# Value windows of a dilated local attention: 64 scratch planes read by 16 large loads instead of 128 small ones, reciprocals spread by ScalarE, and a new order of all steps

## The chip, the cores and the metric

The kernel runs on one core of one Trainium2 chip. A core has five engines that each work through their own instruction queue in order: TensorE (PE, matrix products; its weight loads are shown as PEld), VectorE (DVE), ScalarE (ACT), GpSimd (POOL), and SyncE (SP), which here only issues DMAs. DMAs move data between the chip's DRAM and the on-chip memory SBUF; matrix products land in PSUM, a small accumulator memory. The metric is the device time of one execution in microseconds.

## The reference

There are 2048 tokens of 512 features, all in bfloat16. After a first layernorm (xn) two branches are computed and joined:

```python
def _A_ref(x, wqkv, wo):                      # H = 32 heads of Dh = 16
    W, dil = 8, 2
    qkv = (x @ wqkv) ...                      # q, k, v per head
    idx = pos[:, None] - off[None, :]         # each token sees itself and 2, 4, ... 14 tokens back
    logits = einsum("bhsd,bhswd->bhsw", q, kg) * scale   # 8 logits per token and head
    logits = where(idx >= 0, logits, -1e9)
    attn = softmax(logits)
    o = einsum("bhsw,bhswd->bhsd", attn, vg)  # weighted sum of 8 shifted values
    return o @ wo

def _B_ref(x, w1, w2, w3, w4):
    h = gelu(layernorm(x) @ w1)
    hs = concat(four quarters of h shifted by 1, -1, 2, -2 tokens) @ w2
    x1 = x + hs
    return x1 + gelu(layernorm(x1) @ w3) @ w4    # F = 1376

xn = layernorm(x);  s = _A_ref(xn, ...);  g = silu(_B_ref(xn, ...));  return x + s * g
```

## The kernel before, in words

Tokens are cut into 16 tiles of 128, four tiles to a chunk, four chunks. Small Python functions, called steps, each issue one piece of work for one tile, chunk or column block. A string ORDER (line 16 and following) lists the names of all steps; at the end of the program the steps are called in that order. Every engine therefore gets its own instructions in the sequence of ORDER, and an instruction that waits holds up everything behind it on the same engine. Nothing reorders it later.

The steps, by name (c is a chunk, i a tile):

- x and w steps (SP): loads of inputs and weights; `xc2`, `xc3` are the 512 KB loads of the x rows of chunks 2 and 3.
- `st`, `rsa`, `rsb`, `rsc`, `xn` (lines 261 to 308): first layernorm. Statistics on DVE, the power of -1/2 on POOL (`rsb`), `-mean*rstd` on DVE (`rsc`), and the normalised rows on ACT (`xn`, line 308; for chunk 0 on DVE). `r2a`, `r2b`: the second layernorm's scale, DVE and POOL.
- `tr`, `xe` (PE transposes, then copies) or `tx` (line 339, a DMA transpose issued by SP): xn turned for the products. Chunks 0 and 1 use PE, chunks 2 and 3 the DMA.
- `qk c.n` (line 393), `qe` (line 399): eight products per chunk for q and k, and their evictions on ACT.
- `v i`, `ve i`, `vst i` (lines 405, 411, 416): values of one tile; ACT evicts them with the features of a head interleaved; POOL issues the store to the DRAM scratch `v_dram`, 2062 rows of 1 KB, the first 14 zero.
- `h i`, `he i`, `hst i` (lines 405, 420, 426): first MLP product, gelu on ACT, DMA transpose issued by SP into `hT`. `pl`, `pr_`: two columns on each side copied by POOL. `mix i` (line 553): the product of the shifted quarters with w2. `xo`, `s3` (DVE), `ra3`, `rb3`, `rc3`, `xm` (ACT), `x1T` (DMA transpose, SP): x1, its layernorm and its turned form.
- `pw c.u` (DVE, line 448), `lg c.u` (PE, line 457): q times k shifted by 2u, and the sum over the 16 features of a head by a product with a 0/1 matrix, for the eight shifts u. PSUM tile `lg` holds 8 x 128 logits for (tile of the chunk, head) on the partitions.
- `mask`, `mx`, `ls`, `ex`, `to`, `sh`, `et`, `ae` (lines 462 to 514): softmax over the eight shifts, then eight PE transposes (`et`) and a copy (`ae`) that bring the weights to partitions (shift within a half, token within 32). In `sh` DVE takes the reciprocals, casts them and multiplies.
- `lv i.half` (line 655): loads of the shifted values of one tile, four DMAs of 128 KB for each half of the shifts, issued by SP, each to 32 partitions. `pr i` (DVE, line 661): values times weights, 4096 elements per partition. `ws i` (PE, line 670): the sum over shifts by a 0/1 matrix `sel`. `oe` (ACT, line 676), `oTe` (DMA transpose by SP, line 690; in the last three tiles PE and ACT, `ot`), `wo i` (line 715): the output product.
- `w3 c.f`, `ge` (lines 608, 615): 11 blocks of the hidden layer with gelu on ACT; `w4 i` (line 623): 11 matmuls per tile; `yy` (DVE), `si` (ACT silu). `sg`, `fa` (DVE), `out` (store by SP): joining and output; the last tile in two halves.

Buffers bound how far a step can run ahead: 3 value tiles (`vsp`), 3 tiles of evicted values (`vcp`), 2 of `pw`, 6 PSUM tiles of one rotating set, 4 turned outputs (`oTp`), 2 `o_sb`.

Of the kernel before, what the change touches and what calls it, by code (L numbers as in the profile page):

```python
# [16 lines left out]
warm0 sel x1 qa0 x0 x2 w1 x3 root wqk0 wqk1 st0 wv st1 xc1 rsa0 w2 xn0 rsa1 st2 tr0 xe0 xn1 rsa2 st3 wo.0 h0  # L17
xn2 rsa3 tr1 xn3 tr2 xe1 xe2 tr3 r2a0 h1 xe3 r2q0 h2 r2b0 he0 h3 v0 he2 hst0 qk0.6 ve0 st6 he1 qk0.0 vst0 w3.1
st7 qe0.6 pl0 hst1 v2 qe0.0 st4 qk0.3 ve2 st5 hst2 vst2 he3 rsa1.0 qe0.3 rsb1.0 lv0.0 v1 qk0.5 ve1 rsc1.0 r2a1
xn6 qk0.2 vst1 hst3 qe0.5 r2b1 qk0.1 xn4 xc3 qe0.2 mix1 lv0.1 qe0.1 qk0.7 xn5 xo1 xn7 qk0.4 s31 xc2 qe0.7  # L20
tr1.0 qe0.4 lv1.0 tr1.1 xe1.0 mix0 qa1 pw0.0 h4 xe1.1 lv1.1 v5 he4 xo0 qk1.2 st12 ve5 qk1.7 vst5 s30 hst4
qe1.2 st11 lg0.0 qe1.7 qk1.0 lv2.0 pl1 st8 h7 qe1.0 st10 qk1.4 w4.1 he7 st9 qk1.5 lv2.1 pw0.2 qe1.4 pr_0 h5
qe1.5 rsa2.0 st14 rsb2.0 qk1.6 he5 hst7 st15 v3 qe1.6 rsc2.0 hst5 st13 xn8 mix2 r2a2 ve3 v4 tx8 rsa3.0 xn10
r2b2 pw0.1 mix3 xn9 tx10 xo2 rsb3.0 ve4 v7 xo3 xn11 qk1.1 vst4 s32 tx9 ve7 vst3 rsc3.0 qk1.3 r2a3 qe1.1 vst7
w3.0 s33 xn15 lg0.2 r2b3 tx11 lg0.1 pw0.7 qe1.3 h6 xn12 mix4 ra30 he6 pw0.5 rb30 xn13 h8 hst6 xo4 xn14 v8 rc30
s34 he8 v6 xm2 hst8 h10 ve8 ve6 vst8 tx12 lg0.7 xm0 lg0.5 vst6 pw0.4 v10 he10 pl2 x1T0 xm3 h9 pw0.6 ve10 pr_1
tx13 h11 he9 vst10 lg0.6 he11 lg0.4 tx15 mix5 pw0.3 mix7 x1T2 pw1.0 qa2 v11 tx14 xo7 qk2.7 ve11 xo5 w3.3 qk2.1
vst11 s37 qe2.7 w3.2 v13 s35 qe2.1 hst10 xm1 qk2.3 ve13 x1T3 lg0.3 qe2.3 qk2.2 vst13 mask x1T1 qk2.4 pw1.1
# [24 lines left out]
"""


@with_exitstack
def kernel(
# [18 lines left out]
    W = 8  # L76
# [723 lines left out]
```

## Time and profile before

| quantity | value |
|---|---|
| median of 3 runs | 201.24 us (200.54 to 204.09) |
| the profiled execution, own time | 202.74 us |
| its span, first to last instruction | 201.0 us |
| PE busy | 187.4 us, 93% |
| DVE busy | 165.6 us, 82% |
| ACT busy | 132.5 us, 66% |
| POOL busy | 30.8 us, 15% |
| mean granted TensorE clock | 0.989 |
| DMA queue of SP | 56416 packets, 33.24 MB |

Busy times are sums of instruction durations in the span. An instruction's duration is slightly longer than the distance to the next one on the same engine, since they overlap. The granted clock is the share of its full rate that TensorE was allowed. "To landing" of a DMA counts from its issue to its completion. The profiled execution is 1.5 us above the median of the runs, so differences are worked out against it and carried over to the median.

### The profile page before, as it was taken

Reading aid. Unit: us, or ns where it says so; the run is one execution under the profiler, and the core shown is the slowest. Engines: PE = TensorE matmul, PEld = TensorE weight load, DVE = VectorE, ACT = ScalarE, POOL = GpSimd, SP = SyncE. Lnnn points to the kernel's source line nnn. Section 1 sums busy time; section 2 is a strip of 40 time slices with the busy share of each in tenths; the row PEclk is TensorE's granted clock in tenths of the full one; section 3 lists DMA queues with packets and bytes.
Section 4 is the critical chain, followed back from the end, with each engine's and each line's share of the span. In section 5 each row is a group of like instructions: output and inputs, shape, how many; then the busy total and the mean of one; then the engine's idle time right before and its main releaser. Section 6 shows DMA issues by size and latency. Waiting matters only on the chain.

```text
span 201.0 us, 3994 instructions
## 1 busy us (share of the span) xinstructions
PE 187.4 (93%) x1470; PEld 90.0 (45%) x1496; DVE 165.6 (82%) x265; ACT 132.5 (66%) x204; POOL 30.8 (15%) x48
## 2 busy tenths in 40 slices
PE   7599999939999999999999999999999999999991
PEld 7344544413444444454444444445444444444440
DVE  5752667993496799997999999899999999689854
ACT  3498856595837799727689639497446629953370
POOL 4015220692731411120000020000020000000000
PEclk9999999996999999999999999999999999999999
DMA  5988999999699654766985446666937567798302
GB/s 186 343 260 188 256 248 256 253 141 243 153 108 258 165 169 95 203 144 179 224 215 139 116 126 181 176 116 172 252 76 203 129 138 186 215 258 248 93 29 79
DMA packets 57908, 36.27 MB, mean 180 GB/s; under 512 B 31794, under 2 KB 56864, under 8 KB 57888
## 3 DMA queue, kind: packets, MB, share of 16 engines
q1 hardware_dynamic: 56416, 33.24, 67.8%
q0 software_dynamic: 800, 2.11, 3.2%
q10 hardware_dynamic: 672, 0.66, 1.0%
q8 instruction: 12, 0.20, 0.4%
q14 instruction: 8, 0.07, 0.2%
HBM read 24.84 MB, written 4.21 MB: 145 GB/s over the span
## 4 chain that ended last, share of the span: by engine, by line
PE 86%; DMA 4%; ACT 4%; DVE 3%; issue 1%; ACTq 0%; DVEq 0%
PE w_ps L608 19%; PE w_ps L623 19%; PE qk_ps L393 13%; PE v_ps L405 7%; PE w_ps L553 6%; PE h_ps L405 6%; PE wo_ps L715 6%; PE lg L457 4%; PE o_ps L670 4%; DMA xnT<-xn 3%; DMA x_all<-in_A_x_dram 1%; DVE stats L262 1%; PE et_ps L506 1%; ACT vct L411 1%; ACT xn L308 1%
## 5 line engine op out<-in xcount | busy, mean ns | idle before, releaser
L448 DVE TENSOR_TENSOR pw<-qT,kT 128x2048 bf16<-128x2048 bf16 x32 | 38.2, 1216 | 5.3 <-PE lg L457 5.1
L608 PE MATMUL w_ps<-x1nT,w_sb 128*128 128x512 bf16 (+1 forms) x168 | 41.1, 380 | 0.4
L623 PE MATMUL w_ps<-w_sb,h3t 128*128 128x512 bf16 (+1 forms) x171 | 39.4, 379 | 0.5 <-issue 0.3
L661 DVE TENSOR_TENSOR vs<-vs,att 128x4096 bf16<-128x4096 bf16 x16 | 36.3, 2287 | 0.2
L615 ACT ACTIVATE h3t<-w_ps 128x512 bf16<-128x512 f32 (+1 forms) x44 | 25.1, 605 | 12.9 <-PE w_ps L608 12.6
L393 PE MATMUL qk_ps<-xnT,wqk_sb 128*128 128x512 bf16 x122 | 30.4, 379 | 0.5 <-issue 0.3
L623 PEld LDWEIGHTS <-h3t 128*128 128x128 bf16 (+1 forms) x176 | 16.7, 98 | 20.7 <-issue 0.8
L608 PEld LDWEIGHTS <-w_sb 128*128 128x128 bf16 (+1 forms) x176 | 16.9, 100 | 19.1 <-DMA vs<-v_dram 0.4
L405 PEld LDWEIGHTS <-xnT 128*128 128x128 bf16 x128 | 12.6, 101 | 16.8 <-issue 2.3
L553 PE MATMUL w_ps<-w_sb,hT 128*128 128x512 bf16 x63 | 16.2, 379 | 3.6 <-DMA hT<-ht 3.6
L393 PEld LDWEIGHTS <-wqk_sb 128*128 128x128 bf16 x128 | 12.2, 98 | 14.9 <-issue 0.4
L676 ACT ACTIVATE o_sb<-o_ps 128x512 bf16<-128x512 f32 x16 | 9.5, 598 | 12.8 <-DMA oT<-o_sb 3.7
L405 PE MATMUL v_ps<-wv_sb,xnT 128*128 128x512 bf16 x62 | 17.2, 398 | 0.1
L405 PE MATMUL h_ps<-w_sb,xnT 128*128 128x512 bf16 x61 | 16.0, 393 | 1.0 <-ACT xnT L334 0.7
L632 ACT ACTIVATE g<-g 128x512 bf16<-128x512 bf16 x16 | 10.0, 629 | 10.1 <-DVE g L629 10.0
L262 DVE BATCH_NORM_STATS2 stats<-x_all 128x6 f32<-128x512 bf16 x16 | 10.8, 675 | 4.7 <-DMA x_all<-in_A_x_dram 4.7
L715 PE MATMUL wo_ps<-wo_sb,oT 128*128 128x512 bf16 x59 | 14.5, 379 | 0.2
L416 POOL DMA_DIRECT2D v_dram<-vct x16 | 9.0, 563 | 36.5 <-ACT vct L411 36.5
L420 ACT ACTIVATE ht<-h_ps,rstd 128x512 bf16<-128x512 f32 x16 | 10.9, 687 | 5.0 <-issue 2.0
L571 POOL TENSOR_TENSOR rstd<-ve,mhalf 128x4 f32<-128x4 f32 x4 | 4.3, 1067 | 58.4 <-DVE ve L566 58.4
L580 ACT ACTIVATE xn<-x,nmr,rstd 128x512 bf16<-128x512 bf16 x16 | 13.1, 819 | 0.0
L629 DVE TENSOR_TENSOR g<-w_ps,x 128x512 bf16<-128x512 f32 x16 | 10.7, 681 | 2.8 <-PE w_ps L623 2.8
(84 smaller groups left out, 234.0 us busy)
## 6 DMA issues: line engine op xcount, KB each, us to landing
vs<-v_dram SPq DMA_DIRECT2D x128, 128.0 KB, 3.0
v_dram<-vct POOLq DMA_DIRECT2D x16, 128.0 KB, 2.9
out_dram<-x_all SPq DMA_DIRECT2D x15, 128.0 KB, 2.5
x_all<-in_A_x_dram SPq DMA_DIRECT2D x3, 512.0 KB, 7.0
w_sb<-in_B_w_dram SPq DMA_DIRECT2D x4, 344.0 KB, 3.9
w_sb<-in_B_w_dram SPq DMA_DIRECT2D x2, 640.0 KB, 5.9
wqk_sb<-in_A_wqkv_dram SPq DMA_DIRECT2D x2, 512.0 KB, 6.4
w_sb<-in_B_w_dram ACTq DMA_DIRECT2D x1, 512.0 KB, 4.9
```

Source lines behind the costliest of these rows:

```text
L262: nc.vector.bn_stats(out=stats1[:, i, :], in_=x_all[:, i, :])
L393: nc.tensor.matmul(pt, lhsT=wqk_sb[:, dt, nt * P : (nt + 1) * P], rhs=xnT_t[c][:, dt, :], start=(dt == 0), stop=(dt == ND - 1))
L405: nc.tensor.matmul(pt, lhsT=xnT_t[c][:, dt, jj * P : (jj + 1) * P], rhs=w_sb[:, dt, :], start=(dt == 0), stop=(dt == ND - 1))
L420: nc.scalar.activation(ht_t[i], ps.pop(f"h{i}"), AF.Gelu_apprx_tanh, scale=rstd2[:, i : i + 1])
L448: nc.vector.tensor_tensor(out=pw, in0=q_t[c], in1=k_t[c][:, :, DIL * u : DIL * u + CH], op=ALU.mult)
L553: nc.tensor.matmul(pt, lhsT=hT_t[c][:, g, b0 + shift[g] : b0 + shift[g] + P], rhs=w2_sb[:, g, :], start=(g == 0), stop=(g == ND - 1))
L580: nc.scalar.activation(xn3_t[i], x1_t[i], AF.Identity, bias=nmr3[:, i : i + 1], scale=rstd3[:, i : i + 1])
L608: nc.tensor.matmul(pt[:fs, :], lhsT=w3_sb[:, dt, ft * P : ft * P + fs], rhs=x1nT_t[c][:, dt, :], start=(dt == 0), stop=(dt == ND - 1))
L615: nc.scalar.activation(h3_t[c, ft][:fs, :], ps.pop(f"w3{c}.{ft}")[:fs, :], AF.Gelu_apprx_tanh)
L623: nc.tensor.matmul(pt, lhsT=h3_t[c, ft][:fs, jj * P : (jj + 1) * P], rhs=w4_sb[:fs, ft, :], start=(ft == 0), stop=(ft == NF - 1))
L661: nc.vector.tensor_tensor(out=vv, in0=vv, in1=at_t[c][:, :, jj, :].unsqueeze(2).to_broadcast([P, NB * 2, DH, H]), op=ALU.mult)
L715: nc.tensor.matmul(pt, lhsT=oT[:, dt, :], rhs=wo_sb[:, dt, :], start=(dt == 0), stop=(dt == ND - 1))
```

## The change

Four things change together.

- **The scratch for values.** `v_dram` becomes 64 planes of 65 rows of 1 KB. Token 32q + r is stored twice: in plane 32 + r, row q, and in plane r, row q + 1. A plane read along its rows therefore steps by 32 tokens, and a shift of the token moves to another plane. Each `vst` step issues two stores on POOL instead of one.
- **The loads.** They go by pairs of tiles: `lv p.half` is one DMA of 1 MB. A partition stands for (token within 32, one of four shifts) and takes 8 KB that lie in one run: eight blocks of 32 tokens. The source has the token as its outer dimension of 32 and the shift as the next, of 4. There are 16 such DMAs in place of 128. A product `pr p.half` waits for one load; the sum `ws p.a` (a = tile of the pair) needs the products of both halves. Still three value buffers of the same size, now one per half of a pair. The turned outputs are kept per pair (`oTp` 2 in place of 4 tiles); the last pair, tiles 14 and 15, uses PE and ACT for its turn, where the last three tiles did.
- **Softmax layout.** Exponentials are written as (half, token, shift); sums and weights follow. The reciprocal moves to the end of `to`; a new step `sd` on ACT writes it in bfloat16 four times over, and `sh` multiplies on DVE in place. The mask of the first chunk is one DVE addition of a prepared tile in place of seven memsets; POOL prepares that tile with eight memsets at the start.
- **ORDER.** The whole list is new, from the loads on. The step names of the attention are per pair; the other steps are the same ones in another sequence. Among others, `xc3` moves ahead of `hst1`, the statistics of chunk 3 ahead of those of chunk 2, and `w4.1` far back.

The diff, cut to its core (of ORDER the stretches around the first chunk change, and the end):

```diff
 ORDER = """
-warm0 sel x1 qa0 x0 x2 w1 x3 root wqk0 wqk1 st0 wv st1 xc1 rsa0 w2 xn0 rsa1 st2 tr0 xe0 xn1 rsa2 st3 wo.0 h0
-xn2 rsa3 tr1 xn3 tr2 xe1 xe2 tr3 r2a0 h1 xe3 r2q0 h2 r2b0 he0 h3 v0 he2 hst0 qk0.6 ve0 st6 he1 qk0.0 vst0 w3.1
...
-qe1.2 st11 lg0.0 qe1.7 qk1.0 lv2.0 pl1 st8 h7 qe1.0 st10 qk1.4 w4.1 he7 st9 qk1.5 lv2.1 pw0.2 qe1.4 pr_0 h5
-qe1.5 rsa2.0 st14 rsb2.0 qk1.6 he5 hst7 st15 v3 qe1.6 rsc2.0 hst5 st13 xn8 mix2 r2a2 ve3 v4 tx8 rsa3.0 xn10
-r2b2 pw0.1 mix3 xn9 tx10 xo2 rsb3.0 ve4 v7 xo3 xn11 qk1.1 vst4 s32 tx9 ve7 vst3 rsc3.0 qk1.3 r2a3 qe1.1 vst7
-w3.0 s33 xn15 lg0.2 r2b3 tx11 lg0.1 pw0.7 qe1.3 h6 xn12 mix4 ra30 he6 pw0.5 rb30 xn13 h8 hst6 xo4 xn14 v8 rc30
...
-wo12 oTe14 si13 ws15 sg12 ot13 oe15 wo14 fa12 oTe13 out12 ot15 sg14 wo13 oTe15 fa14 wo15.0 sg13 out14 wo15.1
-sg15.0 fa13 out15.0 sg15.1 out13 out15.1
+warm0 sel x1 qa0 x0 x2 w1 x3 root wqk0 wqk1 st0 wv st1 xc1 rsa0 w2 xn0 rsa1 st2 tr0 xe0 xn1 rsa2 st3 h0 xn2
+rsa3 tr1 xn3 tr2 xe1 xe2 tr3 r2a0 h1 xe3 wo.3 r2q0 h2 r2b0 he0 h3 v0 he1 hst0 qk0.0 ve0 st4 he2 qk0.5 vst0 xc3
+st6 qe0.0 qk0.6 hst1 qe0.5 st7 pl0 v1 qe0.6 st5 hst2 he3 rsa1.0 ve1 rsb1.0 qk0.7 hst3 st13 v3 vst1 qe0.7 r2a1
+v2 rsc1.0 ve3 st14 r2b1 xn4 mix0 st15 ve2 vst3 qk0.2 xc2 xn6 st12 xn5 qk0.4 lv0.0 vst2 xo0 xn7 lv0.1 rsa3.0
+mix2 s30 rsb3.0 qe0.2 tr1.0 qe0.4 xo2 tr1.1 qa1 xe1.0 mix1 wo.0 s32 h4 xe1.1 qk0.1 rsc3.0 he4 st10 xn13 h7
+hst4 xo1 qe0.1 v7 st8 he7 w4.2 pl1 xn14 s31 qk1.0 hst7 ve7 r2a3 qk1.1 qe1.0 st9 vst7 xn15 h6 st11 qe1.1 r2b3
+qk0.3 lv1.0 he6 rsa2.0 xn12 v5 hst6 rsb2.0 qe0.3 h5 ve5 pw0.0 pr_0 qk1.5 vst5 he5 rsc2.0 pw0.1 v4 xn8 hst5
+xn11 qk1.6 r2a2 tx8 ve4 r2b2 lg0.0 qe1.5 qk1.7 pw0.3 qe1.6 tx11 vst4 xn10 mix3 qe1.7 tx10 qk1.3 xo3 lg0.3 s33
...
+yy5 pw3.7 x1T10 si5 to2 w46 xm11 yy4 sd2 x1T11 mix13 yy6 xm9 w47 sh2 si6 x1T9 xo13 si4 s313 mix12 yy7 et2 si7
+xo12 ws3.0 ae2 lg3.0 oe3.0 ws3.1 s312 lg3.7 oe3.1 lv4.1 mix14 pr4.0 oTe3.0 w32.9 lv5.0 w32.0 ge2.9 oTe3.1 xo14
+w32.8 pw3.4 w32.5 ge2.8 s314 ge2.0 w32.7 ge2.5 pr4.1 w32.3 ge2.7 wo6 ge2.3 w32.1 sg6 pw3.1 ws4.0 ge2.1 ws4.1
...
+w33.5 pr6.1 ge3.6 w33.9 ge3.5 w33.2 ge3.9 pr6.0 w33.0 ge3.2 wo11 ge3.0 wo9 pr7.0 ws6.0 ws6.1 oe6.0 w415 lv7.1
+oe6.1 sg9 oTe6.0 sg11 fa9 fa11 oTe6.1 w413 yy15 out9 si15 out11 w412 pr7.1 yy13 w414 yy12 si13 si12 ws7.0 yy14
+ws7.1 oe7.0 wo13 si14 oe7.1 ot7.0 sg13 wo12 oTe7.0 fa13 ot7.1 sg12 wo14 out13 oTe7.1 fa12 wo15.1 sg14 out12
+wo15.0 sg15.1 fa14 out15.1 sg15.0 out14 out15.0
 """
...
+    NQ = S // T32 + 1
...
-    v_dram = dram.tile([PADK + S, D], BF16, name="v_dram")
+    v_dram = dram.tile([2 * T32, NQ, D], BF16, name="v_dram")
...
+    maskb = const.tile([P, W, PADK], F32, name="maskb")
...
-    nc.gpsimd.dma_start(out=v_dram[0:PADK, :], in_=zrows[0:PADK, :])
+    nc.gpsimd.memset(maskb[:], 0.0)
+    for u in range(W - 1):
+        nc.gpsimd.memset(maskb[0:T32, u, 0 : PADK - DIL * u], -1e9)
+    nc.gpsimd.dma_start(out=v_dram[T32 - PADK : T32, 0, :], in_=zrows[0:PADK, :])
...
         def v_s(i):
-            nc.gpsimd.dma_start(out=v_dram[PADK + i * P : PADK + (i + 1) * P, :], in_=vc_t.pop(i))
+            vt = vc_t.pop(i)
+            nc.gpsimd.dma_start(
+                out=v_dram[T32 : 2 * T32, i * NB : (i + 1) * NB, :].rearrange("m q d -> q m d"), in_=vt)
+            nc.gpsimd.dma_start(
+                out=v_dram[0:T32, i * NB + 1 : (i + 1) * NB + 1, :].rearrange("m q d -> q m d"), in_=vt)
...
         def mask():
-            for u in range(W - 1):
-                nc.vector.memset(lg_t[c][0:32, u, 0 : PADK - DIL * u], -1e9)
+            nc.vector.tensor_tensor(
+                out=lg_t[c][:, :, 0:PADK], in0=lg_t[c][:, :, 0:PADK], in1=maskb[:], op=ALU.add)
...
         def expo():
-            Ec_t[c] = smp.tile([P, W, P], BF16, name="E_c", tag="E_c")
-            nc.scalar.activation(Ec_t[c], lg_t.pop(c), AF.Exp)
+            Ec_t[c] = ep.tile([P, 2, P, U4], BF16, name="E_c", tag="E_c")
+            nc.scalar.activation(
+                Ec_t[c], lg_t.pop(c).rearrange("p (a u) t -> p a t u", u=U4), AF.Exp)
 
         def total():
             E_c = Ec_t[c]
-            s4 = smp.tile([P, 4, P], F32, name="s4", tag="s4")
-            nc.vector.tensor_tensor(out=s4, in0=E_c[:, 0:4, :], in1=E_c[:, 4:8, :], op=ALU.add)
+            s4 = smp.tile([P, P, U4], F32, name="s4", tag="s4")
+            nc.vector.tensor_tensor(out=s4, in0=E_c[:, 0, :, :], in1=E_c[:, 1, :, :], op=ALU.add)
             for n in (2, 1):
                 nc.vector.tensor_tensor(
-                    out=s4[:, 0:n, :], in0=s4[:, 0:n, :], in1=s4[:, n : 2 * n, :], op=ALU.add)
-            sm_t[c] = s4[:, 0, :]
+                    out=s4[:, :, 0:n], in0=s4[:, :, 0:n], in1=s4[:, :, n : 2 * n], op=ALU.add)
+            rinv = sm_t[c] = smp.tile([P, P], F32, name="rinv", tag="rinv")
+            nc.vector.reciprocal(out=rinv, in_=s4[:, :, 0])
+
+        def spread():
+            rinv_b = smp.tile([P, P, U4], BF16, name="rinv_b", tag="rinv_b")
+            nc.scalar.activation(
+                rinv_b, sm_t[c].unsqueeze(2).to_broadcast([P, P, U4]), AF.Copy)
+            sm_t[c] = rinv_b
 
         def share():
-            rinv = smp.tile([P, P], F32, name="rinv", tag="rinv")
-            nc.vector.reciprocal(out=rinv, in_=sm_t.pop(c))
-            rinv_b = smp.tile([P, P], BF16, name="rinv_b", tag="rinv_b")
-            nc.vector.tensor_copy(out=rinv_b, in_=rinv)
-            E_n = E_t[c] = ep.tile([P, NB, W, T32], BF16, name="E_n", tag="E_n")
+            E_n = E_t[c] = Ec_t.pop(c)
             nc.vector.tensor_tensor(
-                out=E_n,
-                in0=Ec_t.pop(c).rearrange("p u (b t) -> p b u t", t=T32),
-                in1=rinv_b.rearrange("p (b t) -> p b t", t=T32).unsqueeze(2).to_broadcast([P, NB, W, T32]),
-                op=ALU.mult)
+                out=E_n, in0=E_n,
+                in1=sm_t.pop(c).unsqueeze(1).to_broadcast([P, 2, P, U4]), op=ALU.mult)
...
         def at_e():
-            at_t[c] = attp.tile([P, NB * 2, TPC, H], BF16, name="att", tag="att")
+            at_t[c] = attp.tile([P, 2, TPC, NB, H], BF16, name="att", tag="att")
             nc.vector.tensor_copy(
-                out=at_t[c].rearrange("p n j h -> p n (j h)"),
-                in_=ps.pop(f"et{c}").rearrange("p b u q -> p (b u) q"))
+                out=at_t[c], in_=ps.pop(f"et{c}").rearrange("p u b (j h) -> p u j b h", h=H))
 
...
         def load_vs(uh):
-            if uh == 0:
-                vs_t[i] = vsp.tile([P, NB, 2, D], BF16, name="vs", tag="vs")
-            vs = vs_t[i]
-            for u in range(U4 * uh, U4 * uh + U4):
-                r0 = i * P + DIL * u
-                nc.sync.dma_start(
-                    out=vs[T32 * (u % U4) : T32 * (u % U4) + T32, :, u // U4, :],
-                    in_=v_dram[r0 : r0 + P, :].rearrange("(b t) d -> t b d", t=T32))
-
-        def prod():
-            vv = vs_t[i].rearrange("p b u (dh h) -> p (b u) dh h", dh=DH, h=H)
+            vs_t[p, uh] = vsp.tile([P, 2 * NB, D], BF16, name="vs", tag="vs")
+            m0 = T32 - PADK + DIL * U4 * uh
+            rows = v_dram[m0 : m0 + T32 + DIL * (U4 - 1), 2 * NB * p : 2 * NB * (p + 1), :]
+            src = bass.AP(
+                tensor=rows.tensor, offset=rows.offset,
+                ap=[[NQ * D, T32], [DIL * NQ * D, U4], [1, 2 * NB * D]])
+            nc.sync.dma_start(out=vs_t[p, uh].rearrange("q r d -> q (r d)"), in_=src)
+
+        def prod(uh):
+            vv = vs_t[p, uh].rearrange("q r (dh h) -> q r dh h", dh=DH, h=H)
+            at = at_t[c][:, uh, 2 * k : 2 * k + 2, :, :].rearrange("q j b h -> q (j b) h")
             nc.vector.tensor_tensor(
-                out=vv, in0=vv,
-                in1=at_t[c][:, :, jj, :].unsqueeze(2).to_broadcast([P, NB * 2, DH, H]), op=ALU.mult)
-
-        def gather():
-            vs = vs_t.pop(i)
-            pt = ps[f"o{i}"] = mm_tile("o_ps")
+                out=vv, in0=vv, in1=at.unsqueeze(2).to_broadcast([P, 2 * NB, DH, H]), op=ALU.mult)
+
+        def gather(a):
+            pt = ps[f"o{p}.{a}"] = mm_tile("o_ps")
             for uh in range(2):
-                for b in range(NB):
+                for s in range(4):
                     nc.tensor.matmul(
-                        pt[T32 * b : T32 * b + T32, :], lhsT=sel[:], rhs=vs[:, b, uh, :],
-                        start=(uh == 0), stop=(uh == 1), tile_position=(0, T32 * b))
-
-        def o_e():
-            o_t[i] = op.tile([P, D], BF16, name="o_sb", tag="o_sb")
-            nc.scalar.activation(o_t[i], ps.pop(f"o{i}"), AF.Copy)
-
-        def ot():
-            pt = ps[f"ot{i}"] = mm_tile("ot_ps", (P, ND, P), BF16)
-            o_sb = o_t.pop(i)
+                        pt[T32 * s : T32 * s + T32, :], lhsT=sel[:], rhs=vs_t[p, uh][:, 4 * a + s, :],
+                        start=(uh == 0), stop=(uh == 1), tile_position=(0, T32 * s))
...
```

## The prediction

> **What bounds the kernel now.** First the engine table and the slices of the span.
>
> ```profile
> span 201.0 us, 3994 instructions
> PE 187.4 (93%) x1470; PEld 90.0 (45%) x1496; DVE 165.6 (82%) x265; ACT 132.5 (66%) x204; POOL 30.8 (15%) x48
> ...
> PE   7599999939999999999999999999999999999991
> ```
>
> PE is nearly always busy; there is one hole, about 40 to 45 us, beside the start and the end. The chain that ended last says the same: 86% PE. So only three things can shorten the kernel: that hole, the end, and PE work taken away. Next the hole, by the chain in order of time, the waits, and a table by windows (busy us of PE, PEld, DVE, ACT, POOL, then granted clock, DMA share, GB/s).
>
> ```profile
> 40.69 0.24 ACT xn L308
> 40.93 5.42 DMA xnT<-xn
> 46.34 0.05 issue
> 46.39 1.75 PE h_ps L405 x4
> 48.14 2.05 PE v_ps L405 x5
> ```
>
> ```profile
> PE w_ps L553 <- DMA hT<-ht: 3.6, 1, 3.6
> ```
>
> ```profile
> 42.00:46.00 4.00, 0.61 (x3) 0.21 (x3) 3.49 (x8) 4.00 (x7) 3.98 (x5) 1.00 0.93 184
> 46.00:50.00 4.00, 3.83 (x11) 1.32 (x10) 1.60 (x4) 1.68 (x4) 0.46 (x1) 0.57 1.01 219
> 70.00:105.00 35.00, 34.68 (x302) 16.41 (x297) 33.02 (x41) 26.45 (x41) 3.23 (x6) 1.00 0.69 175
> 105.00:140.00 35.00, 34.52 (x310) 16.71 (x314) 33.98 (x43) 26.36 (x37) 1.04 (x1) 1.00 0.57 146
> 140.00:175.00 35.00, 34.58 (x299) 16.30 (x303) 33.70 (x47) 21.30 (x32) 1.01 (x1) 1.00 0.68 170
> ```
>
> `mix4` stands 3.56 us for the transpose `hst5`, `h8` another 0.17 for `tx8`. Then the granted clock is 0.57: four matmuls take 1.75 us and five 2.05, where the same groups elsewhere take 0.86 and 1.08, so 1.9 us more. **The hole costs 3.6 + 0.2 + 1.9 = 5.7 us.** From 70 to 175 PE has no gap, and DVE is busy 94 to 97%: an order that lets PE run on must not give DVE more to do.
>
> The Trainium skill, "TensorE: Matmul & The Clock Gate", Part 1, says that an idle window of about 3.4 us halves the clock until a busy one has passed. The trace agrees: 3.56 us idle, then clock 0.57. By it a new gap under 3.4 us may cost its own length alone.
>
> **PE's positions.** In the chain a step of four 512-column matmuls takes 0.864 us, a `w4` tile 2.38, one `lg` 0.28, `et` 0.45, a gather `ws` 0.49. I add these along ORDER from `h1` at 10.22. For the kernel before, `mix4` comes out at 41.3 (trace 41.45), and all later shifts are the hole (`h10` 44.8 against 50.84), 0.6 at 66.5 (a wait for `vct`), and 0.5 in crumbs. So a sum of steps places PE to a few tenths. Over the whole list it is 181.0 us before and 180.8 after (one `ot` fewer): **-0.25**.
>
> **The change, part by part.**
>
> *Loads.* 128 issues at a median 0.43 us (line 655) are 55 us of SP; 16 at 0.43 to 3.4 (eight old ones) are 7 to 54. I take 0.5, as the 512 KB and 640 KB loads show 0.43 to 0.58. In the hole SP was the late one: from 24.88 to 37.5 it issued 20 value DMAs, with `hst7` and `hst5` behind them and 640 KB of `w4.1`; `hst5` landed 6.5 us after issue. A 1 MB load lands, by 343 GB/s (best slice) plus the shortest landing of 2.3, in 5.4 us; by 640 KB in 7.4 us scaled, 11.8. I take 5.5 to 6, near the first, as most of these loads stand alone on their queue. Each load has cover: `lv4.1` is released at `ws3.1` (131 + shift) and `pr4.1` starts 7 us later; `lv7.1` follows `ws6.1`, 8 us ahead of its use by `pr7.1`. Queued behind the loads on SP are `oTe` transposes with 8 us and more to spare.
>
> *The hole in the new order.* `mix4` is at 43.6 and `h8` at 42.2. On ACT, from `he4` at 27 on, evictions at a pitch of 0.5, `xn` at 0.7 and `he` at 0.57 put `he5` at 35 and `xn8` at 36. SP then has `hst5` at 35.2, `tx8` at 36.5, each 1.2 to 1.3 to issue. With the landings of this stage (3.2 median, 7.3 worst) `hst5` lands at 38.5 to 42.5, `tx8` at 40 to 44. One 1 MB load (`lv1.0`, about 31) is ahead, `w4.1` is gone. **The hole goes: -5.7**, of which 0 to 2 may stay.
>
> *What is late next.* `st13` stands in DVE's queue behind `rsa1.0`, which DVE reaches at 15.7; it needs `xc3`, which SP issues behind `hst0` at 14.4. The two loads of this size took 5.4 and 7.0 us at 22 to 31 under a DMA share near 1; at 13 to 16 the share is about 0.5, so 4.5: `xc3` lands at 18.9. Waiting behind `st13` on DVE are `r2a1` and `rsc1.0`, so `xn4`, `xn5` on ACT, and `st14`, `st15`, `st12`, `xo0`, `s30`, `xo2`, `xe1.0`: 0.85 + 0.5 + 0.15 + 3 x 0.8 + 0.65 + 0.15 + 0.8 + 0.65 + 0.65 = 6.8 us after landing, 25.7. `h4` needs it at 24.9: **+0.9**, from 0 (landing 18) to 4.7 (8.3 us, the longest landing of an x load).
>
> *Stores.* 32 issues at 0.563 instead of 16: 9 us more on POOL, which is busy 15%. `rsb3.0` and `rsb2.0` stand behind `vst2` and `vst7`; each comes 0.56 to 1.7 later, included above (`rsb2.0` ends at 34 for `rsc2.0` at 35). Three `vct` buffers come free later: 0 to 1 us of ACT, which has gaps; I take 0.
>
> The Trainium skill, "DMA: Bandwidth & Descriptors" (section on why a DMA increments its semaphore by 16), has a rule against these stores: a DMA is spread over the largest number of engines up to 16 that divides the slowest dimension on both sides, and the stores' destination now has 4 there. No row here shows it: a store of 128 KB lands in 2.9 us at the median, and its queue's 3.2% of 16 engines' span is 6 engine-us per store, 0.4 us on 16 engines and 1.5 on four. By the rule `vct` would come free some 2 us later and the upper end above, 1 us, would hold: a sum of -4.2 instead of -5.2.
>
> *DVE and ACT.* Out: seven memsets 0.5, four casts at 0.226 (line 493) 0.9. In: one addition on 8 x 14 f32, from 0.15 (128x4, line 285) to 0.69 (128x512, line 559); I take 0.25. DVE **-1.1 us**. `share`, `total`, `ae` and `pr` keep element counts and types; reading in strides of 128 costs nothing in `mx` (1217 against 1228 for the straight `ls`), so 0; if the short inner runs (4) slow `to` or `sh`, at most twice 0.69 + 0.72 + 0.69 per chunk, +2.1 each. ACT: four spreads, 0.29 (128x4) to 1.02 (`ex`), taken 0.6 as any 512-wide row; and in ORDER the changes of function table count 17 instead of 19, at 1.283: together -0.2. The new wait: `sh` on DVE waits for `sd` on ACT, 0.6 plus what ACT has ahead; for chunk 2 `xm9`, hence `x1T9` and `w32.9`, stand behind `sd2`: by the rows `x1T9` lands about 1 us before `w32.9` needs it.
>
> *Joins in 70 to 175.* With pitches of 1.12 (`pw`), 2.21 (`pr`), 0.62 (evictions), 0.8 (`s3`) and 1.15 (`mx`, `ls`), DVE added along ORDER meets each join before PE does, but by little: `ws0` 0.6, `et1` 1, `ws2` 1, `ws4` 0.9 us. I allow **+1.0** for joins missed by tenths, 0 to 4.
>
> *The end.* Before, the last `w4` matmul ends at 191.35 and the last DVE instruction at 198.30, with a chain of six ACT pieces between: 6.95. After, behind `w414` come `ws7` (0.98), three `wo`, two `ot`: `wo14` ends 4.0 later, and the same DVE row of pieces (195.96 to 198.30, 2.34) follows: 6.3. **-0.65**; between -1.5 and +1 (if `pr7.1`, 4 us ahead, is late).
>
> **The sum**: -5.7 + 0.9 - 0.25 + 1.0 - 0.65 = -4.7, minus about 0.5 for DVE relieved and crumbs: **-5.2 us** on a profiled execution of 202.74 (span 201.0 and 1.7 around it), so 197.5; on the median of 201.24 it gives **196.0**.
>
> **Rivals.**
>
> 1. *A wait takes the hole's place* (chance 0.20). `xc3` lands 7 us after issue, or joins on DVE miss by 3 to 5 us in all. For it: DVE at 97%, margins under 1 us, and x loads that took up to 8.3. Then 4 instead of 0.9, plus 1.9 for the clock if the gap passes 3.5: 200 to 201, within 2%.
> 2. *DMA stays late anyway* (0.10): the transposes, 1.2 us each on SP and one after the other from 35 on, and not the loads, were the limit at 41. For it: after 41 only 55 to 150 GB/s were moved while three `tx` were on their way. Half of the hole stays: 199.
> 3. *The scratch is guarded too coarsely* (0.13, slower). Loads and stores now touch interleaved planes. If a load waits for every store issued before it and a store for every load before it, `lv0.0`, `vst2`, `lv0.1`, `vst7` follow one another: 5 us per load and 4 per store from 26 on put `vst7` at 40, and `rsb2.0` behind it on POOL at 43 instead of 34. `rsc2.0`, `xn8`, `tx8`, `pw0.1` come 8 to 9 us late, and the clock halves: +8 + 2, so 206. It decides as soon as `lv0.0` waits for `vst3`. Against it: today's windows overlap too, and SP waited for stores only 0.3 us.
> 4. *The value product loses its rate* (0.03, slower): at the 1.19 ns per element of `mx`, 4.87 instead of 2.29 us, 16 times: +41, about 237. Against: its inner runs stay 32 long.
>
> **Chances.** The forecast 0.54. Faster by over 2% (under 197.2): 0.54. Within 2%, about what a measurement here can tell from no change: rivals 1 and 2, 0.30. Slower: rivals 3 and 4, 0.16. The range leaves out 4 and most of 3, and takes the floor without new waits (-7.7: 193.5): 193.5 to 204.5. The forecast's own is 194 to 197.2.
>
> **What would show it.** PE busy within 1 us of 187 minus the 2 us of slow clock; no wait of `mix4` or `h8` over 1 us; clock 1.0 in all windows from 10 to 185. A wait of DVE `stats` for `x_all` of about 3 us near 16, and one of PE for `xnT` under 2 us near 25. DVE busy near 164.5. Landing of the 1 MB loads under 7 us; POOL 38 to 41 us busy. From the last `w4` to the last DVE instruction 6.3. Wrong if PE stops over 2 us anywhere between 10 and 185, if `L661` differs from 2287 ns, or if SP waits for `v_dram` stores beyond the first load.

## The result and the profile after

| | before | after |
|---|---|---|
| median of 4 runs each | 202.44 us | 214.82 us |
| the profiled execution, its span | 202.74, 201.0 us | 212.22, 210.4 us |
| mean granted TensorE clock | 0.989 | 0.98 |

The change makes the kernel slower: the ratio is 1.0596, with a 95% interval of 1.0439 to 1.0752. The forecast, 196.0 with a range to 204.5, had the wrong sign. In spans it expected -5.2 us and got +9.4.

The page of the kernel after: engine table and the 40 slices.

```profile
span 210.4 us, 3844 instructions
PE 188.8 (90%) x1466; PEld 89.4 (42%) x1492; DVE 165.3 (79%) x255; ACT 131.8 (63%) x205; POOL 44.9 (21%) x72
...
PE   7597699976994899999999999999999799999991
```

Before there was one hole. Now there are several, all ahead of 90 us but for a small one at 168. The timeline of PE names them (only its rows from 10 us on with a stop over 1 us are shown); the columns are start, busy us, and in brackets the idle time ahead and what ended it.

```profile
21.91 0.82 PE L564 MATMUL w_ps<-w_sb,hT 128*128 128x512 bf16 x3 [1.97 <-DMA hT<-ht]
...
25.90 0.82 PE L564 MATMUL w_ps<-w_sb,hT 128*128 128x512 bf16 x3 [1.06 <-DMA hT<-ht]
...
49.14 1.89 PE L410 MATMUL h_ps<-w_sb,xnT 128*128 128x512 bf16 x4 [3.15 <-DMA xnT<-xn]
...
65.54 1.02 PE L564 MATMUL w_ps<-w_sb,hT 128*128 128x512 bf16 x4 [1.10 <-ACT vct L416]
...
68.83 1.78 PE L398 MATMUL qk_ps<-xnT,wqk_sb 128*128 128x512 bf16 x4 [2.27 <-ACT vct L416]
...
168.00 0.41 PE L466 MATMUL lg<-pw,e_log 128*32 128x128 bf16 x16 [1.04 <-DVE pw L457]
```

Three wait for DMA transposes. The two at 65 and 69 wait for ACT, and ACT waits for stores, as its row in the waits shows (total us, times, longest):

```profile
ACT vct L416 <- DMA v_dram<-vct: 6.4, 2, 3.7
```

So ACT stands until a `vct` buffer has been stored. The chain that ended last, in order of time, has the same transfers, each far longer than the 3 us of before:

```profile
18.66 7.20 DMA hT<-ht
...
30.14 7.78 DMA hT<-ht
38.03 0.04 ACT ht L429
...
38.61 1.42 ACT xn L313 x2
40.03 9.06 DMA xnT<-xn
49.09 0.05 issue
49.14 1.89 PE h_ps L410 x4
...
56.36 8.43 DMA v_dram<-vct
```

The delays add up. `h4` starts at 28.32, late by the two PE stops for `hT` (1.97 and 1.06 us), and with it `he4` on ACT (29.43). Then a late `hT` transpose holds a buffer that the gelu `he5` (`ht`) needs, and ACT stands 1.04 us for it, until 38.03. Behind `he5` are `xn8` on ACT and `hst5` on SP, so `tx8` starts at 40.03, takes 9 us, and `h8` stands. By windows (busy us of PE, PEld, DVE, ACT, POOL, then clock, DMA share, GB/s):

```profile
40.00:50.00 10.00, 6.75 (x61) 2.93 (x60) 5.27 (x8) 7.96 (x14) 7.00 (x7) 0.92 1.32 171
50.00:60.00 10.00, 9.89 (x114) 4.61 (x115) 7.95 (x11) 3.17 (x5) 4.17 (x8) 0.91 1.06 137
60.00:70.00 10.00, 6.63 (x32) 2.73 (x29) 6.27 (x10) 3.22 (x6) 3.46 (x6) 0.95 1.13 147
70.00:105.00 35.00, 34.01 (x308) 15.78 (x313) 28.33 (x28) 28.62 (x45) 8.18 (x11) 0.97 0.96 216
105.00:140.00 35.00, 34.65 (x277) 16.23 (x280) 33.68 (x44) 21.98 (x32) 1.83 (x2) 1.00 0.58 164
140.00:175.00 35.00, 33.75 (x311) 15.86 (x313) 32.75 (x43) 20.75 (x32) 2.98 (x1) 1.00 0.60 166
```

From 105 on PE runs nearly as before. From 40 to 70 the DMA engines count as busy all the time (1.06 to 1.32) and move only 137 to 171 GB/s; before, in these three windows, it was 1.25, 0.79 and 0.82 at 197, 131 and 208 GB/s. The DMA part of the page says which transfers are late (KB each where it is given, median us to landing; the row of `q0`, the queue of the DMAs that POOL issues, has packets, MB and share):

```profile
q0 software_dynamic: 4640, 4.26, 10.2%
...
vs<-v_dram SPq DMA_DIRECT2D x16, 1024.0 KB, 7.2
v_dram<-vct POOLq DMA_DIRECT2D x32, 128.0 KB, 6.6
...
hT<-ht SPq DMA_TRANSPOSE x16, 6.7
x1nT<-xn SPq DMA_TRANSPOSE x16, 2.5
oT<-o_sb SPq DMA_TRANSPOSE x14, 5.5
...
xnT<-xn SPq DMA_TRANSPOSE x8, 6.9
```

The same rows before:

```profile
v_dram<-vct POOLq DMA_DIRECT2D x16, 128.0 KB, 2.9
...
hT<-ht SPq DMA_TRANSPOSE x16, 3.2
...
xnT<-xn SPq DMA_TRANSPOSE x8, 3.5
```

Stores, `hT` and `xnT` take twice as long. All three run in the first half, while values are stored; `x1nT`, which runs mostly later, is as fast at the median as before (2.5 against 2.6). And the transpose at 18.66 landed at 25.85, while the first 1 MB load was issued only at 25.5: the loads can't have delayed that one.

### The profile page after: what moved, and what is told of

Same layout as the page of the kernel before. It is cut to its first block, busy times and chain, and to the rows that moved or that the text cites. A ratio compares the mean times of both kernels' runs of the same rounds, so it can differ in the third digit from the quotient of the medians.

```text
span 210.4 us, 3844 instructions
## 1 busy us (share of the span) xinstructions
PE 188.8 (90%) x1466; PEld 89.4 (42%) x1492; DVE 165.3 (79%) x255; ACT 131.8 (63%) x205; POOL 44.9 (21%) x72
## 3 DMA queue, kind: packets, MB, share of 16 engines
q0 software_dynamic: 4640, 4.26, 10.2%
## 4 chain that ended last, share of the span: by engine, by line
PE 33%; DMA 22%; DVE 18%; issue 17%; ACT 5%; POOLq 1%; POOL 1%; another core or an unknown queue 1%; ACTq 0%; DVEq 0%
PE w_ps L634 11%; DMA hT<-ht 9%; PE w_ps L619 7%; DMA xnT<-xn 4%; DVE vs L672 4%; DMA v_dram<-vct 4%; DMA x1nT<-xn 4%; DVE pw L457 3%; PE h_ps L410 3%; PE w_ps L564 3%; DVE g L748 2%; PE wo_ps L743 2%; PE o_ps L679 2%; PE lg L466 2%; DVE stats L573 2%
## 5 line engine op out<-in xcount | busy, mean ns | idle before, releaser
L672 DVE TENSOR_TENSOR vs<-vs,att 128x4096 bf16<-128x4096 bf16 x16 | 36.2, 2286 | 3.7 <-DMA vs<-v_dram 3.6
L398 PE MATMUL qk_ps<-xnT,wqk_sb 128*128 128x512 bf16 x123 | 32.1, 388 | 2.6 <-ACT vct L416 2.3
L422 POOL DMA_DIRECT2D v_dram<-vct x16 | 11.5, 717 | 43.0 <-ACT vct L416 38.5
L410 PE MATMUL h_ps<-w_sb,xnT 128*128 128x512 bf16 x62 | 16.6, 396 | 3.9 <-DMA xnT<-xn 3.1
L591 ACT ACTIVATE xn<-x,nmr,rstd 128x512 bf16<-128x512 bf16 x16 | 12.4, 806 | 7.6 <-DVE nmr L585 4.3
L582 POOL TENSOR_TENSOR rstd<-ve,mhalf 128x4 f32<-128x4 f32 x4 | 7.2, 1790 | 46.9 <-DVE ve L577 46.9
L416 ACT ACTIVATE vct<-v_ps 128x512 bf16<-128x512 f32 x16 | 9.6, 600 | 11.4 <-DMA v_dram<-vct 6.4
L410 PE MATMUL v_ps<-wv_sb,xnT 128*128 128x512 bf16 x60 | 16.3, 392 | 0.2
L570 DVE TENSOR_TENSOR x<-w_ps,xn 128x512 bf16<-128x512 f32 x16 | 10.8, 679 | 4.3 <-PE w_ps L564 4.3
```

Of the source, the lines that this page charges most:

```text
L398: nc.tensor.matmul(pt, lhsT=wqk_sb[:, dt, nt * P : (nt + 1) * P], rhs=xnT_t[c][:, dt, :], start=(dt == 0), stop=(dt == ND - 1))
L410: nc.tensor.matmul(pt, lhsT=xnT_t[c][:, dt, jj * P : (jj + 1) * P], rhs=w_sb[:, dt, :], start=(dt == 0), stop=(dt == ND - 1))
L422: nc.gpsimd.dma_start(out=v_dram[T32 : 2 * T32, i * NB : (i + 1) * NB, :].rearrange("m q d -> q m d"), in_=vt)
L591: nc.scalar.activation(xn3_t[i], x1_t[i], AF.Identity, bias=nmr3[:, i : i + 1], scale=rstd3[:, i : i + 1])
L672: nc.vector.tensor_tensor(out=vv, in0=vv, in1=at.unsqueeze(2).to_broadcast([P, 2 * NB, DH, H]), op=ALU.mult)
```

## The experiments

**Theory 1**: the shape of the stores holds up every DMA: their destination has 4 outer steps (blocks of 32 tokens) and 32 inner ones (planes). **Theory 2**: it is the bytes, the number of stores or their scattered rows. **Theory 3**: it is the new loads. **Theory 4**: it is the new order. Two bases: the kernel before with two extra stores per tile into unused scratch (labels b_), and the kernel after with one part altered (a_). Intervals are 95%; "before" was 202.1 to 203.1 us beside all of them.

### The shape alone, in the old order

Extra stores of plane shape (first part of the diff), the same bytes in 1 KB rows far apart with 32 outer steps (second), and the same bytes in contiguous rows (third); of the two stores per tile the first and third part show one:

```diff
+            nc.gpsimd.dma_start(
+                out=x_dram[T32 : 2 * T32, i * NB : (i + 1) * NB, :].rearrange("m q d -> q m d"), in_=vt)
...
+    x_dram = dram.tile([2 * T32, 4 * NT + 1, D], BF16, name="x_dram")
+                nc.gpsimd.dma_start(
+                    out=x_dram[T32 * g : T32 * (g + 1), 0 : 4 * NT, :]
+                    .rearrange("a (b s) d -> a b s d", b=4)[:, :, i, :], in_=vt)
...
+            nc.gpsimd.dma_start(out=x_dram[i * P : (i + 1) * P, :], in_=vt)
```

> The kernel before, and for every value tile two more stores on POOL of the shape that the changed kernel uses (four groups of 32 rows of 1 KB, each row into another plane), into a scratch that nobody reads. Theory 1 (the shape of the plane stores holds up all DMA): 6 us or more above the kernel before, hT and xnT transposes land in 6 to 9 us between 20 and 70 as in the changed kernel. Theory 2 (only the added bytes and POOL issues): the same rise as with two contiguous stores. Theory 3 (the 1 MB loads are the cause): within 2 us of before. Theory 4 (the new order of steps): within 2 us of before.

> As the run with plane stores, same bytes and also 1 KB rows far apart, but the slowest dimension of the destination is 32 (32 groups of 4 rows) and not 4. If the number of engines that a slowest dimension of 4 allows is what hurts: within 2 us of before, and store landings near 3 us. If scattered 1 KB rows hurt whatever the grouping: the same rise as with the plane stores, 6 us or more.

> The kernel before with two more contiguous stores of 128 KB for every value tile, into a scratch that nobody reads: same bytes, same POOL issues (32 more at about 0.56 us). Theory 2 (bytes and POOL time): as far above before as the run with plane stores. Theories 1, 3, 4: within 2 us of before.

Measured: planes 222.51 us (1.1001, 1.0887 to 1.1116); 32 outer steps 203.58 (1.0105, 0.9998 to 1.0212); contiguous 203.89 (1.0142, 1.0064 to 1.0219). So bytes, issues and scattered rows cost about 1%, at most 2.2, and the plane shape 19 us, without any large load and in the old order. `hT` lands in 6.3 us with the planes and in 4.7 with 32 outer steps (3.2 before).

### What in the shape

First attempt: 2, 4 and 8 outer steps over rows 16 KB apart (here 4):

```diff
+    x_dram = dram.tile([8, 32 * NT, D], BF16, name="x_dram")
+                    out=x_dram[4 * g : 4 * (g + 1), :, :]
+                    .rearrange("a (b s) d -> a b s d", b=32)[:, :, i, :], in_=vt)
```

> The kernel before with two extra stores per value tile into unused scratch, the destination cut as 8 groups of 16 scattered rows of 1 KB. If a store is carried by as many engines as its slowest dimension has entries, 8 engines carry it: half the added load per engine of the plane-shaped extra stores (222.5 us, against 203.6 for 32 groups), so between the two and nearer to the lower, 204 to 211. If any destination of scattered groups under 16 is equally bad, 217 to 225; if only the plane shape is bad, 203 to 205.

> As the one with 8 groups, with 4 groups of 32 scattered rows of 1 KB: the same bytes, the same 1 KB rows far apart as with 32 groups of 4 rows (203.6 us); only the grouping differs. By the slowest dimension alone it is as slow as the plane-shaped stores: 217 to 227. If what hurts is something else in the planes (rows of different partitions next to each other), it stays at 203 to 206.

> As the one with 8 groups, with 2 groups of 64 scattered rows. By the slowest dimension two engines carry 32 x 128 KB: twice the load per engine of 4 groups, which added some 19 us; at about 6 engine-us per store the two get 96 us each on top of what they carry anyway: 235 to 265. If the number of groups does not matter below 16, 217 to 227.

Measured: 203.07, 204.84 and 203.50 us (ratios 1.0134, 1.0175, 1.0145), none slower than 32 outer steps by more than 1.3 us. This looks like a refutation and is a fault of the design: an outer step of 32 x 16 KB continues the inner one evenly, so the destination is 128 rows at one stride and the groups don't exist. The queue row shows it in all three: 2336 packets, as with 32 outer steps. One row of padding keeps the groups apart (first part, for 4; likewise 2 and 8); a fourth kernel (second part) stores to exactly the addresses of the one with 32 outer steps, in the order of the planes:

```diff
-    x_dram = dram.tile([8, 32 * NT, D], BF16, name="x_dram")
+    x_dram = dram.tile([8, 32 * NT + 1, D], BF16, name="x_dram")
...
-                    .rearrange("a (b s) d -> a b s d", b=4)[:, :, i, :], in_=vt)
+                    .rearrange("a (b s) d -> b a s d", b=4)[:, :, i, :], in_=vt)
```

> As the one with 4 padded groups, 8 groups of 16 rows. By the number of groups, half the added load per engine of 4 groups: 205 to 213. If the number does not matter: 203 to 206.

> Two extra stores per value tile, 4 groups of 32 rows, rows 16 KB apart and the groups kept apart by a row of padding, so that they cannot be one even stride. Slowest dimension 4 with descending strides. By the number of groups alone: 217 to 227. If only an inner step that is larger than the outer one hurts: 203 to 206.

> As the one with 4 padded groups, 2 groups of 64 rows. By the number of groups, twice the added load per engine of 4 groups: 235 to 265. If the number does not matter: 203 to 206.

> The kernel before with two extra stores per value tile to exactly the addresses of the 32-group kernel (203.6 us), met in the order of the planes: 4 outer steps of 16 KB, 32 inner steps of 65 KB, all rows apart. If a slowest dimension of 4 is what hurts: as the planes, 217 to 227, and the stores land in about 6.9 us. If the planes hurt because rows of four partitions lie side by side (1 KB apart): 203 to 206, stores in about 4.

Measured: 8 outer steps 208.38 us (1.0337, 1.0218 to 1.0456), 4 steps 224.65 (1.106, 1.0806 to 1.1315), 2 steps 245.45 (1.2158, 1.1947 to 1.2369), the turned one 224.85 (218.82 to 225.94). All four lie where the number of outer steps puts them. The DMA part of the page with 32 outer steps (packets, MB and share of the software queue; then KB each and median us to landing):

```profile
q0 software_dynamic: 2336, 6.31, 10.7%
...
x_dram<-vct POOLq DMA_DIRECT2D x32, 128.0 KB, 4.1
...
hT<-ht SPq DMA_TRANSPOSE x16, 4.7
```

With 8 padded steps:

```profile
q0 software_dynamic: 3360, 6.33, 13.4%
...
x_dram<-vct POOLq DMA_DIRECT2D x32, 128.0 KB, 5.5
...
hT<-ht SPq DMA_TRANSPOSE x16, 5.9
```

With 4 padded steps:

```profile
q0 software_dynamic: 5408, 6.36, 15.1%
...
x_dram<-vct POOLq DMA_DIRECT2D x32, 128.0 KB, 7.3
...
hT<-ht SPq DMA_TRANSPOSE x16, 6.5
```

With 2 padded steps:

```profile
q0 software_dynamic: 9504, 6.42, 18.5%
...
x_dram<-vct POOLq DMA_DIRECT2D x32, 128.0 KB, 9.9
...
hT<-ht SPq DMA_TRANSPOSE x16, 8.4
```

The store lands later with fewer steps, and so does a transpose that has nothing to do with it. With the same addresses and bytes in both kernels (32 steps and turned), only the cut and the order of the rows that comes with it can be the cause; the padded kernels keep the rows in ascending order and are as slow, so it is the cut. The Trainium skill, "DMA: Bandwidth & Descriptors" (section on why a DMA increments its semaphore by 16), has a rule that would give the reason: a transfer is put on the largest number of engines, up to 16, that divides the slowest dimension of both sides. The runs agree in the order 32, 8, 4, 2 of the times (203.6, 208.4, 224.7, 245.5).

The profiles don't name the engine of a packet, but the packet records in the traces show how many of the software queue's 4 KB data packets were under way at once. The most frequent number is 16 in the kernel before (1.9 us of the run) and with 32 outer steps (4.8 us), 8 with 8 padded steps (7.8), 4 with the turned stores (14.8), 2 with 2 padded steps (18.4), and 4 in the kernel after (14.2). With 4 padded steps it is 8 (9.0), then 5 and 4, as if two stores often ran side by side. These counts fit a store that is carried by as many streams as it has outer steps, up to 16. How such a store makes a transpose late is not seen packet by packet; that it does is what the landings above show.

### The shape undone in the new order

**Stride-4 tiles.** A value tile takes every fourth token of a chunk in place of 128 in a row, by a stride in the product's operand. Its store then has 16 outer steps and 8 inner ones; count, bytes, planes, loads and issuing engine stay. `lv0.0` moves behind `vst2`, because a tile now reaches all blocks of its chunk.

```diff
+                    cols = xnT_t[c][:, dt, :].rearrange("p (a r) -> p r a", r=TPC)[:, jj, :]
...
-                out=v_dram[T32 : 2 * T32, i * NB : (i + 1) * NB, :].rearrange("m q d -> q m d"), in_=vt)
...
+                planes = v_dram[m0 : m0 + T32, q1 : q1 + CH // T32, :].rearrange("(a r) q d -> r q a d", r=TPC)
+                nc.gpsimd.dma_start(out=planes[r], in_=vt)
```

> The changed kernel with another cut of the same plane stores: tile r of a chunk now holds every fourth token (r, r + 4, ...), so its destination has a slowest dimension of 16 (blocks) instead of 4, with eight rows of 1 KB in each, every row in another plane. Same number of stores, bytes and POOL issues; lv0.0 moves behind vst2, which it needs now. Theory 1 (a slowest dimension of 4 holds up all DMA): store landings fall from 6.6 to about 4 us, the transposes to 3 to 5, and the time to 195 to 203; if the sum of the prediction held otherwise, 196. Theory 4 (the new order or the large loads are slow by themselves): 209 to 215.

Measured: 206.08 us (1.0184, 1.0081 to 1.0287), against a ratio of 1.0596 for the kernel after: some 8 us less. That is between the 195 to 203 expected of theory 1 and the 209 to 215 of theory 4. The DMA part of its page, queue, stores and transposes:

```profile
q0 software_dynamic: 1568, 4.21, 7.0%
...
v_dram<-vct POOLq DMA_DIRECT2D x32, 128.0 KB, 4.0
...
hT<-ht SPq DMA_TRANSPOSE x16, 4.2
```

4640 - 1568 = 3072 packets are gone, 96 per store, as many as the 4 padded steps had more than the 32: (5408 - 2336) / 32 = 96. One stop over 1 us is left behind 10 us; its row in PE's timeline:

```profile
55.10 2.12 PE L413 MATMUL v_ps<-wv_sb,xnT 128*128 128x512 bf16 x5 [3.41 <-issue]
```

The row names no releaser. It is `v12`, which now needs all four turned tiles of chunk 3, while `tx14` is issued only at 52.2 and lands 2.8 us later, at 55.0: the stop belongs to this variant.

**That stop removed**: `tx14` right behind `tx13`, and `v12` and `v9` change places (with their `ve` and `vst`).

```diff
-mix4 tx15 pw0.7 xm1 mix5 pw0.2 tx13 he8 v8 ...
-vst10 mix6 tx14 pw0.5 he9 v12 ...
+mix4 tx15 pw0.7 xm1 mix5 pw0.2 tx13 tx14 he8 v8 ...
+vst10 mix6 pw0.5 he9 v9 ...
```

> The kernel after the change with the stride-4 value tiles, and tx14 moved ahead of hst8, v12 changed places with v9, so that v12 no longer waits for a late tx14. Theory (stores with a slowest dimension of 4 were the cause, and the stop of 3.4 us with its slow clock at 55 us was an artefact of the stride-4 tiles): 5.5 us less than the 206.1 of the stride-4 kernel, 199 to 202, 1 to 2% faster than before, no stop of PE over 1.5 us between 10 and 185. Rival (another transfer is late next, the new order needs more of DMA than it gets): the stop moves to h13 or mix7 and the time stays at 203 to 206.

Measured: 200.60 us against 202.14 before, ratio 0.9993 (0.9955 to 1.003), so no difference from before that can be told, and by the ratios 12 us less than the kernel after. The stop went as expected; the 1 to 2% below before that were expected too did not come. The profiled execution takes 199.91 us; its engine table and slices:

```profile
span 198.0 us, 3847 instructions
PE 186.3 (94%) x1466; PEld 90.2 (46%) x1492; DVE 165.0 (83%) x255; ACT 131.7 (66%) x205; POOL 39.2 (20%) x72
...
PE   7599999999999999999999999999999799999990
```

PE has no stop over 1 us behind 10 us. Against the kernel after, the span is 12.4 us shorter: 2.5 of it PE busy time, the rest PE idle time (21.6 against 11.7).

### Other queues, other loads

**Each plane store in four of 32 rows, issued by SP**, and **plane stores issued by ACT**:

```diff
+            for q in range(NB):
+                vq = vt[T32 * q : T32 * q + T32, :]
+                nc.sync.dma_start(out=v_dram[T32 : 2 * T32, i * NB + q, :], in_=vq)
+                nc.sync.dma_start(out=v_dram[0:T32, i * NB + q + 1, :], in_=vq)
...
-            nc.gpsimd.dma_start(
+            nc.scalar.dma_start(
```

> The changed kernel with every plane store cut into four of 32 rows, slowest dimension 32, issued by SP instead of POOL (8 per tile at about 0.45 us, 58 us of SP in all, near what the 112 loads took away). Same bytes in the same places. Theory 1: the transposes land in 3 to 5 us again and the time falls to 197 to 204. Theory 3 or 4 (loads or order): stays within 4 us of the changed kernel, 209 to 215.

> The changed kernel with its plane stores, shape unchanged (slowest dimension 4), issued from the queue of ACT instead of POOL, 32 issues at about 0.46 us more on ACT (63% busy). If the shape hurts on any queue: stays at 209 to 216. If it is the descriptors made by POOL that hurt: 198 to 204.

The quarters: 247.15 us (1.2266, 1.215 to 1.2382), far from what I expected. Transposes are quick again, as the DMA part of its page shows:

```profile
v_dram<-vct SPq DMA_DIRECT2D x128, 32.0 KB, 1.7
...
hT<-ht SPq DMA_TRANSPOSE x16, 3.1
```

but 128 stores, 0.42 us of SP each at the median, now stand in SP's queue in front of the transposes, so the cure for the shape is probably paid for in SP's order; no run separates the two. On ACT: 218.58 us (1.0852, 1.076 to 1.0944), above the 209 to 216 expected. Here ACT waits and shape mix, so the pair was also run on the kernel before:

> The kernel before with the two extra plane-shaped stores per value tile, issued by ScalarE in place of GpSimd. The price of the shape is the difference to the same kernel with 32 groups, also issued by ScalarE. If the shape alone sets the price: about the 19 us that GpSimd's pair showed (222.5 against 203.6). If stores from this queue always fall on the same few engines: more than 25. If this queue spreads them in another way: under 5.

> The control of the pair: two extra stores per value tile with 32 groups of 4 rows, issued by ScalarE. 32 issues at 0.5 to 0.7 us on an engine that is busy 66%, and some waiting for values there: 205 to 215.

Planes from ACT 239.23 us (234.26 to 241.52), 32 steps from ACT 214.81 (1.0585, 1.0504 to 1.0666): 24.4 between the medians, 20.6 between the fastest. The shape costs about as much from this queue as from GpSimd's (18.9).

**Loads split** into eight of 128 KB, and **the spread on DVE** instead of ACT, both on the stride-4 kernel:

```diff
+            for b in range(2 * NB):
...
+                nc.sync.dma_start(out=vs_t[p, uh][:, b, :], in_=src)
...
-            nc.scalar.activation(
-                rinv_b, sm_t[c].unsqueeze(2).to_broadcast([P, P, U4]), AF.Copy)
+            nc.vector.tensor_copy(
+                out=rinv_b, in_=sm_t[c].unsqueeze(2).to_broadcast([P, P, U4]))
```

> As the cut by every fourth token, and each 1 MB load split into eight of 128 KB (1 KB per partition), 128 loads again on SP, about 55 us of issue instead of 8. If the large loads hold transposes up: as fast as or faster than the unsplit one. If the prediction is right that SP's issue time was what made transposes late: 3 to 10 us slower than the unsplit one.

> As the cut by every fourth token, and the reciprocals spread by DVE instead of ACT: four copies of 512 f32 to bf16, about 0.6 us each on DVE, and no wait for ACT. If DVE is the tight engine from 70 to 175: 1 to 3 us slower. If DVE has room: within 1 us.

Split loads: 232.37 us (1.1558, 1.1437 to 1.1679), 26 more than with whole ones, and more than expected, though transposes land sooner (`hT` 3.2, `oT` 2.7 against 4.2 and 5.5). So the large loads are not what makes this order slow, which contradicts theory 3; that it is the 128 issues on SP which cost the 26 us is likely and not shown by itself. The spread on DVE: 206.80 against 206.08, no difference that can be told.

## Why the prediction was wrong

**The step that failed is "Stores".** It named the 4 outer steps, worked out 1.5 instead of 0.4 us per store, and asked only who waits for the store itself: three `vct` buffers, 0 to 1 us of ACT, taken as 0. It left out that such a store also delays transfers that have nothing to do with it. Measured: with 16 outer steps and the stop of `v12` removed the span falls by 12.4 us, and the same shape costs 19 us in the old order. The waits for `vct` are a part (stops of 1.10 and 2.27, where 0 to 1 us of ACT was allowed); the larger part are transposes that land after 7 to 9 us (stops of 1.97, 1.06 and 3.15). The rule on the slowest dimension stood in the prediction, priced at 1 us because only the stores' own landing was looked at.

**The hole** took landings of 3.2 to 7.3 us from the stage before, which had no such stores beside it. `tx8` was put at 36.5 and landing at 40 to 44; it was issued at 40.03 and landed at 49.09, because late `hT` transposes had held up PE (1.97 and 1.06 us) and then ACT (1.04). So a stop of 3.15 us and a slow clock came back in the same place. The prediction expected that a gap under 3.4 us may cost its own length alone. Here it did not: behind the 3.15 us four matmuls took 1.89 us and behind the 2.27 us (itself 1.0 us of work after the stop of 1.10) 1.78, where four take 1.03 elsewhere; behind the stops of 1.97 and 1.10 us the clock stayed full. Without the shape the step holds: `h8` stands 0.20 us, `mix4` not at all, and the clock is 1.00 from 10 to 175.

**Loads**: issue 0.54 us at the median (0.5 taken); landing 7.2, not 5.5 to 6, and still 7.0 with cheap stores. Nothing in the order had to wait long for it: DVE stood 3.6 us in all for `vs`.

**POOL**: 44.9 us busy, 38 to 41 forecast: a plane store is issued in 717 and 698 ns, not 563. With stride-4 tiles it is 39.2.

**Right in size**: the join on DVE (+1.0 allowed; 1.04 at 168, 0.96 in the variant with `tx14` moved, here called the last); DVE 165.3 us busy (164.5); the product 2286 ns (2287), so rival 4 is out; the spread 628 ns (0.6); the mask's addition 282 ns (0.25); DVE's wait for `xc3`, 3.53 us at 16.3 (about 3 near 16), behind which `h4` stands 0.35 us in the last variant (0.9); from the last `w4` to the last DVE instruction 6.6 us (6.3).

**Rivals.** Rival 1, a wait in the hole's place, describes what was seen, but its causes (`xc3`, DVE joins) weren't it. Rival 2 was right that transposes would be late and wrong about why. Rival 3 is out: SP waited 2.2 us for stores in two waits. That the kernel came out slower was given a chance of 0.16, all of it for other reasons.

**The sum without the shape** can be held against the last variant, and it does not hold either. The ratio of 0.9993 (0.9955 to 1.003) is a gain of 0.9 us at most, where the sum had 5.2. The two profiled executions look better: span 198.0, forecast by the terms as 195.8, against 201.0 before. Of the 2.2 us, PE busy time is about 1.1 (it fell by 1.1 where the slow clock and one `ot` should have given 2.15); the rest is PE idle time in pieces under 1 us. But these two are not typical: the executions behind the ratio took 199.40 to 202.33 us before and 199.91 to 201.65 with the variant, so the profiled 202.74 lies above all of the former and 199.91 at the bottom of the latter.

So a second step is in doubt: the hole of 5.7 us was measured in one execution, at a mean clock of 0.989, and carried over to the median. Six of the ten executions before ran at 0.996 to 0.999 and took 199.40 to 200.94 us, the other four at 0.987 to 0.989 and took 201.16 to 202.33. That fits a hole without the 1.9 us of slow clock in the six, but none of them was traced, so how much of the hole they had, and where the rest of the forecast gain went, stays open.

## What to carry to other kernels

Before a store is reshaped, look at the outermost step count of its access pattern, after even strides have been merged. Here 16 and 32 steps to the destination were cheap and 8, 4 and 2 were not, and the price was paid by transfers that ran beside the store and not only by the one that waited for it; loads and the source side were not varied. So list all transfers in that stage that something waits for. A packet count per DMA in the queue's row that is well above that of a sibling with the same bytes is the sign to look for. And take the gain from several executions: a hole that one profile shows need not be in the median.

## What the runs showed of the hardware

- 32 stores of 128 KB more cost 1% of the run with 32 outer steps and 3.4, 10.6 and 21.6% with 8, 4 and 2.
- Fewer outer steps bring extra packets: (3360, 5408, 9504 - 2336) / 32 = 32, 96 and 224 per store, that is 32 x (16/g - 1) for g steps. With 4 steps these are 3072 packets of 16 bytes each. What they do isn't shown.
- The number of a queue's data packets under way at once is most often 16, 8, 4 or 2 for stores with 32, 8, 4 (turned) or 2 outer steps.
- `oT` transposes, which run beside the 1 MB loads, land in 5.5 us instead of 2.5, and in 2.7 with the loads split.
